# Down- and output projection of three segments in row tiles that rotate over four PSUM banks, with score fills between them

## The chip, the cores and the metric

The kernel runs on one core of a Trainium2 chip. The metric is the device time of one execution in microseconds, the median of the runs.

## The reference

Two branches work on the same input `x` of 2048 rows and 512 columns (`A_x`); their sum is weighted by a gate per row. Branch A is Infini-attention in four segments of 512 rows with 32 heads of 16 columns, with a running memory `M`, `z` per head. Branch B is a GEGLU feed-forward with 1792 hidden columns.

```python
for s in range(4):                                  # branch A, per segment
    logits = q_s @ k_s.T * 0.25 + causal_mask        # 32 heads, 512 x 512
    a_dot = softmax(logits) @ v_s
    a_mem = (phi(q_s) @ M) / (phi(q_s) @ z + 1e-6)   # phi(t) = t + 1 if t > 0 else exp(t)
    o_s = sigmoid(beta) * a_mem + (1 - sigmoid(beta)) * a_dot
    M, z = M + phi(k_s).T @ v_s, z + phi(k_s).sum()
a = o @ wo
b = (gelu(x @ w_gate) * (x @ w_up)) @ w_down          # branch B
g = sigmoid((x * gate_w).sum(-1))
out = g * a + (1 - g) * b
```

## The kernel before

All work is cut into named tasks, and each of the five queues (TensorE `pe`, ScalarE `act`, VectorE `dve`, GpSimd `pool`, and the DMA queue `sp`) runs its tasks in an order that is written out by hand in `ORDER`. `Sched.schedule` walks these lists only to hand out PSUM banks and to interleave the queues for bookkeeping; its estimates (`SWITCH`, `HOP`, `BLOCK`) do not appear in the program that runs. `Emitter` then derives the semaphore waits from what each instruction reads and writes. Between two TensorE instructions it sets none, as they run in order.

Names say what a task does; the first number is the segment.

- `K`, `Q`, `V` are the projections, `G` and `U` the gate and up projection of one hidden tile of 128 columns. Each has four matmuls over the contraction, in pieces of two (`.0`, `.2`), each matmul 128 by 128 by 512 columns. The results go to one of four PSUM banks `psW`, and ScalarE or VectorE copies them out (`Kev`, `Gev`, `Um` and so on). `gelu` tasks run on ScalarE between the attention phases, since the exponential and gelu need different tables.
- `qk{s}_{t}{A0,B0,L,A1,B1}` is a score fill. Four row tiles of 32 rows (one per head pair group) write into the four banks of `psXALL`, 512 columns each. One exponential `exp` on ScalarE reads all four banks into `pt`, and GpSimd masks the diagonal (`msk`). There are 18 fills a segment, and `psXALL` is held once, so a fill waits for the exponential before it.
- `pv{s}_{t}_{j}` is P times V in column tiles, with transpose `pvt` and normalization `norm` on VectorE into `oT`; `mz` updates the memory in column tiles; `numx` and `num` read it (`numx` in row tiles). `oTd` are DMA transposes of the memory part into `oT`.
- `D{s}_{tile}.{i}` is the joint down- and output projection of 128 rows of the segment: 4 matmuls of `oT` with `wo` and 14 of `hT` with `wd`, 18 in all, accumulated in one `psW` bank; before the change each tile goes through its 18 chunks in nine pieces of two, and the tiles run spread over the next segment's attention. `fin{s}_{tile}` scales the bank by `omgt` into `ostage` on ScalarE or VectorE, and `out` writes it.

TensorE thus works in three tilings: full (128 by 128), row tiles (32 by 128, in the profile `32*128`) and column tiles (`128*32`, `128*17`). `column_runs` looks at each stretch between two row-tiled tasks; where it holds a `pv` or `mz`, the full matmuls of the stretch are also issued as four column tiles each (line 533), so that the stretch has one tiling. Otherwise they are issued as one (line 531).

Segment 3 keeps its own form: its last tile `D3_3` is accumulated in `psXALL` after all scores are done.

Of the kernel before, what the change touches and what calls it, by code (L numbers as in the profile page):

```python
# [16 lines left out]
D = 512  # L17
# [9 lines left out]
N_OST = 3  # L27
PSUM_KEYS = ("X", "W")
# [3 lines left out]
SWITCH = 0.097  # L32
# [54 lines left out]
    ),  # L87
    "act": (
# [15 lines left out]
    ),  # L104
    "dve": (
# [34 lines left out]
    ),  # L140
}
GAP = {DVE: 0.012, POOL: 0.063}
HOP = {PE: 0.25, ACT: 0.07, DVE: 0.07, POOL: 0.10, SP: 0.0}


class Instr:
# [64 lines left out]
class Sched:  # L211
# [48 lines left out]
    def schedule(self):  # L260
# [13 lines left out]
        while len(order) < n:  # L274
# [26 lines left out]
            if e == PE:  # L301
                if st < COLD:
                    t.finish = st + 2 * t.est[e] if 2 * t.est[e] <= COLD - st else COLD + t.est[e] - (COLD - st) / 2
                if t.tiled != mode:
                    t.finish += SWITCH
# [898 lines left out]
```

## Time and profile before

| what | us |
|---|---|
| median of 3 runs (264.21 to 264.8) | 264.63 |
| the profiled execution, own time | 265.65 |
| its span, first to last instruction | 264.4 |
| TensorE busy (matmul) | 259.4 (98%) |
| ScalarE busy | 212.2 (80%) |
| VectorE busy | 196.6 (74%) |
| GpSimd busy | 106.0 (40%) |
| granted TensorE clock | 1.00 |

The profiled execution lies 1.02 us above the median. Matmuls are pipelined, so a matmul's duration is longer than the distance to the next one's start; busy time of TensorE counts any stretch in which one is under way. Line numbers are those of the kernel before. Line 531 is a full matmul, 533 a column-tiled part of one, 906 a score fill, 912 its exponential, 954 and 962 P times V, 873 the memory update, 826 its row-tiled reading, 1053 the multiplication of the up projection into `hT`, 1099 and 1102 the scaled copies of the output.

### The profile page before, as it was taken

The numbers are of one execution on the slowest core, as the hardware profiler recorded it, in microseconds if no ns is written. First come the engines' busy times: TensorE is split into PE (matmuls) and PEld (weight loads), VectorE is DVE, ScalarE is ACT, GpSimd is POOL, SyncE is SP. The second block draws the span as 40 slices with busy tenths as digits, with TensorE's granted clock in tenths as the row PEclk, the third lists the DMA queues.
The fourth block names the chain that finished last, engine by engine and source line by source line (L and its number), as shares of the span: only waits on it lengthen the run. The fifth ranks groups of instructions, "written<-read, shape, count | busy, mean of one in ns | idle before, by whom it ended". The sixth has DMA issues, their size and how long they took to land.

```text
span 264.4 us, 9416 instructions
## 1 busy us (share of the span) xinstructions
PE 259.4 (98%) x4164; PEld 120.0 (45%) x4164; DVE 196.6 (74%) x369; ACT 212.2 (80%) x190; POOL 106.0 (40%) x256
## 2 busy tenths in 40 slices
PE   8799999999999999999999999999999999999996
PEld 4444445344544444544444444543455434454454
DVE  1589998898998978767795877679895765637363
ACT  3589999889999798799968888789986786877822
POOL 8216843815003464461460164256460233316520
PEclk9999999999999999999999999999999999999999
DMA  6973033940006956120003413310002031000102
GB/s 217 282 198 62 4 72 101 331 141 2 5 6 166 170 84 61 44 82 0 2 2 85 71 32 62 103 41 1 4 2 42 2 84 44 12 30 2 42 2 82
DMA packets 32776, 18.37 MB, mean 69 GB/s; under 512 B 20576, under 2 KB 32736, under 8 KB 32736
## 3 DMA queue, kind: packets, MB, share of 16 engines
q1 hardware_dynamic: 31632, 16.73, 27.5%
q10 hardware_dynamic: 1104, 1.05, 1.2%
q8 instruction: 32, 0.52, 0.8%
q14 instruction: 8, 0.07, 0.1%
HBM read 9.84 MB, written 2.10 MB: 45 GB/s over the span
## 4 chain that ended last, share of the span: by engine, by line
PE 91%; DMA 3%; DVE 2%; POOL 2%; ACT 1%; issue 1%; ACTq 0%; DVEq 0%
PE psW L531 47%; PE psW L533 25%; PE psXALL L906 9%; PE psW L954 5%; DMA wk<-in_A_wk_dram 3%; PE psXALL L533 1%; PE psW L962 1%; PE psXALL L531 1%; POOL gbd L681 1%; ACT pt L912 1%; PE psXALL L826 1%; DVE mzbd L892 1%; PE psW L873 0%; POOL pt L915 0%; DVE obf L984 0%
## 5 line engine op out<-in xcount | busy, mean ns | idle before, releaser
L912 ACT ACTIVATE pt<-psXALL 128x2048 bf16<-128x2048 f32 x64 | 120.1, 1876 | 23.2 <-PE psXALL L906 19.8
L915 POOL TENSOR_SCALAR_AFFINE_SELECT pt<-pt 128x256 bf16<-128x256 bf16 x128 | 57.3, 457 | 119.9 <-ACT pt L912 114.9
L1053 DVE TENSOR_TENSOR hT<-psW,hT 128x512 bf16<-128x512 f32 x56 | 37.6, 686 | 19.0 <-PE psW L531 15.0
L968 DVE STREAM_TRANSPOSE tb<-psW 128x512 f32<-128x512 f32 x32 | 22.3, 707 | 19.5 <-PE psW L962 19.3
L531 PE MATMUL psW<-wd,hT 128*128 128x512 bf16 x136 | 35.5, 380 | 0.0
L531 PE MATMUL psW<-xT,wu 128*128 128x512 bf16 x132 | 34.9, 380 | 0.0
L531 PE MATMUL psW<-xT,wg 128*128 128x512 bf16 x138 | 34.0, 379 | 0.0
L915 POOL TENSOR_SCALAR_AFFINE_SELECT ptl<-ptl 128x512 bf16<-128x512 bf16 x32 | 23.2, 726 | 10.9 <-ACT ptl L912 9.3
L906 PE MATMUL psXALL<-qT,kpad 32*128 32x320 bf16 (+3 forms) x512 | 25.4, 273 | 0.0
L533 PE MATMUL psW<-xT,wu 128*32 128x512 bf16 x368 | 22.0, 379 | 0.0
L533 PE MATMUL psW<-xT,wg 128*32 128x512 bf16 x344 | 20.9, 379 | 0.0
L1037 ACT ACTIVATE hT<-psW 128x512 bf16<-128x512 f32 x28 | 15.3, 598 | 6.6 <-PE psW L533 3.5
L813 POOL COPY exsT<-exs 32x4 f32<-32x4 f32 x64 | 14.1, 220 | 15.9 <-ACT exs L804 12.2
L531 PEld LDWEIGHTS psW<-xT,wg 128*128 128x128 bf16 x138 | 12.9, 98 | 16.0 <-DVE hT L554 0.5
L531 PEld LDWEIGHTS psW<-wd,hT 128*128 128x128 bf16 x136 | 12.5, 98 | 15.8 <-issue 2.1
L533 PE MATMUL psW<-wd,hT 128*32 128x512 bf16 x296 | 19.4, 380 | 0.0
L954 PE MATMUL psW<-pt,vaug 128*17 128x192 bf16 (+3 forms) x512 | 19.3, 273 | 0.0
L531 PE MATMUL psW<-xT,wk 128*128 128x512 bf16 (+1 forms) x74 | 17.2, 334 | 2.0 <-DMA wk<-in_A_wk_dram 1.5
L906 PEld LDWEIGHTS psXALL<-qT,kpad 32*128 32x128 bf16 x512 | 7.6, 92 | 24.7 <-ACT pt L912 14.0
L912 ACT ACTIVATE ptl<-psXALL 128x2048 bf16<-128x2048 f32 x8 | 15.0, 1878 | 4.6 <-PE psXALL L906 4.6
L531 PEld LDWEIGHTS psW<-xT,wu 128*128 128x128 bf16 x132 | 11.7, 98 | 14.7 <-issue 1.9
L531 PE MATMUL psW<-wv,xT 128*128 128x512 bf16 x58 | 16.5, 380 | 0.0
(122 smaller groups left out, 372.3 us busy)
## 6 DMA issues: line engine op xcount, KB each, us to landing
out_dram<-ost SPq DMA_DIRECT2D x15, 128.0 KB, 1.8
wg<-in_B_w_gate_dram SPq DMA_DIRECT2D x2, 896.0 KB, 7.9
wu<-in_B_w_up_dram SPq DMA_DIRECT2D x2, 896.0 KB, 7.0
wd<-in_B_w_down_dram SPq DMA_DIRECT2D x2, 896.0 KB, 5.7
phkt<-in_A_x_dram SPq DMA_DIRECT2D x3, 512.0 KB, 3.8
vlow<-vaug SPq DMA_DIRECT2D x8, 136.0 KB, 2.7
hT<-in_A_x_dram SPq DMA_DIRECT2D x2, 256.0 KB, 3.9
wq<-in_A_wq_dram SPq DMA_DIRECT2D x2, 256.0 KB, 6.1
```

What stands on the lines that cost most here:

```text
L531: return e.matmul(view(), lhsT, rhs, start=first, stop=last)
L533: r = e.matmul(view()[c:c + 32, :], lhsT[:, c:c + 32], rhs, start=first, stop=last, tile_position=(0, c))
L681: gb = task("gbd", POOL, [Instr(lambda e, c=c, j=j: e.tensor_tensor(gbd[32 * c:32 * c + 32, :, j, 0:16], gmat[32 * c:32 * c + 32, 2 * c + ...
L813: cross = task(f"exsT{s}", POOL, [Instr(lambda e, g=g, c=c: e.tensor_copy(exsT[sl][32 * g:32 * g + 32, c:16:4], exs[32 * c:32 * c + 32, s4 ...
L826: task(f"numx{s}", PE, [Instr(lambda e, g=g, i=i, qt=qt, t=t: e.matmul(X[g][:, 34 * i:34 * i + 34], phq[32 * g:32 * g + 32, t, qt * 128:(q ...
L906: instrs.append(Instr(lambda e, g=g, lhs=lhs, rhs=rhs, c0=c0, ncol=ncol: e.matmul(X[g][:, c0:c0 + ncol], lhs(32 * g), rhs(32 * g), start=T ...
L912: exp_task(s, f"exp{s}_{t}{name}", [Instr(lambda e: e.activation(dst[:], XALL[:, :].rearrange("p (g c) -> p g c", g=4), ACTF.Exp, scale=AT ...
L915: task(f"msk{s}_{t}{name}", POOL, [Instr(lambda e, view=view, pat=pat, base=base: e.affine_select(out=view, in_=view, compare_op=ALU.is_ge ...
L954: instrs.append(Instr(lambda e, t=t, q=q, kb=kb, slot=slot, c0=c0: e.matmul(gp.f32()[32 * q:32 * q + 17, 128 * kb + 64:512], Vaug[sl][:, k ...
L968: task(f"pvt{s}_{t}_{j}", DVE, [Instr(lambda e: e.transpose(Tb[:, j, :], gp.f32()[:, :]), [gp.key], [("Tb", j)], dve_t(512))], grp=gp)
L1037: lambda e, g=g, ft=ft, s=s: e.activation(hT[s % 2][:, ft, :], g.f32()[:, :], ACTF.Gelu_apprx_tanh),
L1053: task(f"Um{s}_{ft}", DVE, [Instr(lambda e, g=g, ft=ft: e.tensor_tensor(hT[sl][:, ft, :], g.f32()[:, :], hT[sl][:, ft, :], ALU.mult), [g.k ...
```

## The change

For segments 0 to 2 the tiles no longer accumulate one after the other. `row_downs` takes all four banks at once, one per tile. The first two and the last two of the 18 chunks of each tile stay whole matmuls (`D{s}_{tile}.0` and `.16`). The 14 chunks between are cut into four row parts of 32 contraction rows. In step `k` of four, row group `r` works on tile `(r + k) % 4`, so that the four row groups always write four different banks; each piece `R{s}.{step}.{c}` covers two chunks, 8 matmuls. After each step the groups take the next bank; the first matmuls of a step wait on TensorE's own semaphore (`own`) for the matmuls of the step before. As `R` pieces have the tiling of score fills, fills stand between them in the new order without a change of tiling.

The orders of all five queues are written anew. A block now lies in the first third of the next segment's attention, where the up projections of the next segment stood; these move behind it. All other functions keep what they compute. `finish` is the old end of `downs`, moved out. The constants of `Sched` change as well.

```diff
+D_HEAD, D_TAIL = 2, 2
-SWITCH = 0.097
+SWITCH = 0.1
 ...
     "pe": (
 ...
+        "U0_6.2 U1_4.0 U1_4.2 Q2_1.2 U0_13.0 pv0_3_1 U0_13.2 qk1_0B0 D0_1.0 Q2_3.0 Q2_3.2 D0_3.0 qk1_0L D0_0.0 "
+        "D0_2.0 R0.0.2 R0.0.4 qk1_0A1 R0.0.6 R0.0.8 R0.0.10 R0.0.12 R0.0.14 qk1_0B1 R0.1.2 R0.1.4 R0.1.6 R0.1.8 "
+        "R0.1.10 R0.1.12 R0.1.14 qk1_1A0 R0.2.2 R0.2.4 R0.2.6 R0.2.8 R0.2.10 R0.2.12 R0.2.14 qk1_1B0 R0.3.2 R0.3.4 "
+        "R0.3.6 R0.3.8 R0.3.10 qk1_1A1 R0.3.12 R0.3.14 D0_0.16 D0_2.16 D0_1.16 qk1_1B1 pv1_0_1 pv1_0_0 U1_9.0 "
+        "U1_9.2 U1_8.0 qk1_2A0 Q2_2.0 Q2_2.2 D0_3.16 U1_2.0 U1_8.2 qk1_2B0 U1_2.2 U1_11.0 U1_11.2 pv1_1_1 pv1_1_0 "
 ...
+        "qk2_0A0 V2_1.0 Q3_1.0 Q3_1.2 V2_1.2 D1_0.0 D1_3.0 D1_2.0 D1_1.0 R1.0.2 qk2_0B0 R1.0.4 R1.0.6 R1.0.8 "
 ...
+        "G3_12.0 G3_12.2 G3_13.0 G3_13.2 U3_3.0 qk3_0A0 U2_2.0 U3_3.2 U2_2.2 D2_0.0 D2_3.0 D2_1.0 D2_2.0 R2.0.2 "
+        "qk3_0B0 R2.0.4 R2.0.6 R2.0.8 R2.0.10 R2.0.12 R2.0.14 qk3_0L R2.1.2 R2.1.4 R2.1.6 R2.1.8 R2.1.10 qk3_0A1 "
+        "R2.1.12 R2.1.14 R2.2.2 R2.2.4 R2.2.6 qk3_0B1 R2.2.8 R2.2.10 R2.2.12 R2.2.14 R2.3.2 qk3_1A0 R2.3.4 R2.3.6 "
+        "R2.3.8 R2.3.10 R2.3.12 R2.3.14 qk3_1B0 D2_0.16 D2_1.16 D2_2.16 V3_3.0 V3_3.2 qk3_1A1 U3_5.0 U3_5.2 "
 ...
-HOP = {PE: 0.25, ACT: 0.07, DVE: 0.07, POOL: 0.10, SP: 0.0}
+HOP = {PE: 0.235, ACT: 0.07, DVE: 0.07, POOL: 0.10, SP: 0.0}
 ...
                 if d[0] == "c":
-                    if d[1] == PE and eng == PE:
+                    if d[1] == PE and eng == PE and not ins.own:
                         continue
 ...
+    def row_downs(s):
+
+        sl = s % 2
+        gs = tuple(Grp(banks) for _ in range(4))
+
+        def chunk(c, tile):
+            at = slice(tile * 128, (tile + 1) * 128)
+            if c < 4:
+                return oT[sl][:, c, at], wo[:, c, :], [("oT", sl, tile, c), ("w", "wo")]
+            return hT[sl][:, c - 4, at], wd[:, c - 4, :], [("hT", sl, c - 4), ("w", ("wd", (c - 4) // 7))]
+
+        def whole(tile, c0, c1):
+            g = gs[tile]
+            return [mm(g, lambda: g.f32()[:, :], *chunk(c, tile), c == 0, c == 3 + NFT, 512) for c in range(c0, c1)]
+
+        def part(r, tile, c):
+            a, b, rd = chunk(c, tile)
+            return Instr(lambda e: e.matmul(gs[tile].f32()[:, :], a[32 * r:32 * r + 32, :], b[32 * r:32 * r + 32, :],
+                                            start=False, stop=False, tile_position=(32 * r, 0)),
+                         rd, [gs[tile].key], mm_t(512) / 4)
+
+        for tile in range(4):
+            task(f"D{s}_{tile}.0", PE, whole(tile, 0, D_HEAD), grp=gs[tile])
+        c1 = 4 + NFT - D_TAIL
+        for step in range(4):
+            for c in range(D_HEAD, c1, 2):
+                ins = [part(r, (r + step) % 4, cc) for cc in range(c, min(c + 2, c1)) for r in range(4)]
+                t = Task(f"R{s}.{step}.{c}", {PE: ins}, grp=gs)
+                t.tiled, t.row = "qk", True
+                if c == D_HEAD and step > 0:
+                    t.hand = True
+                    for i in ins[:4]:
+                        i.own = True
+                S.add(t)
+        for tile in range(4):
+            task(f"D{s}_{tile}.{c1}", PE, whole(tile, c1, 4 + NFT), grp=gs[tile])
+        for tile in range(4):
+            finish(s, tile, gs[tile])
 ...
     def downs(s):
         sl = s % 2
         last = s == NSEG - 1
+        if not last:
+            return row_downs(s)
```

The scaled copies move as well: of the twelve `fin` tasks of segments 0 to 2, ScalarE runs three (`fin0_1`, `fin2_1`, `fin2_3`) and VectorE nine.

More of the change, by code (lines that the diff above doesn't have):

```diff
@@ L142 @@
 GAP = {DVE: 0.012, POOL: 0.063}
-HOP = {PE: 0.25, ACT: 0.07, DVE: 0.07, POOL: 0.10, SP: 0.0}
+HOP = {PE: 0.235, ACT: 0.07, DVE: 0.07, POOL: 0.10, SP: 0.0}
 class Instr:
-    __slots__ = ("fn", "reads", "writes", "est", "dma_sem", "waits", "deps", "inc", "fence", "wide", "cols")
+    __slots__ = ("fn", "reads", "writes", "est", "dma_sem", "waits", "deps", "inc", "fence", "wide", "cols", "own")
     def __init__(self, fn, reads=(), writes=(), est=0.1, dma_sem=None):
@@ L161, in __init__ @@
         self.fence = False
-        self.wide = self.cols = False
+        self.wide = self.cols = self.own = False
 class Grp:
@@ L190, in __init__ @@
         self.alts = alts
-        self.grps = () if grp is None else (grp,)
+        self.grps = () if grp is None else grp if isinstance(grp, tuple) else (grp,)
         self.after = tuple(after)
@@ L195, in __init__ @@
         self.tiled = None
+        self.row = self.hand = False
         self.table = None
@@ L281, in schedule @@
                     continue
-                st = max(cur[e], ready_at[t.id])
+                st = max(cur[e] + (SWITCH if e == PE and t.tiled != mode else 0.0), ready_at[t.id])
                 if t.grps and t.grps[0].bank is None:
@@ L303, in schedule @@
                     t.finish = st + 2 * t.est[e] if 2 * t.est[e] <= COLD - st else COLD + t.est[e] - (COLD - st) / 2
-                if t.tiled != mode:
-                    t.finish += SWITCH
                 mode = t.tiled
@@ L332, in schedule @@
                 npred[s.id] -= 1
-                hop = 0.0 if (e == PE and s.alts.keys() == {PE}) else HOP[e]
+                hop = 0.0 if e == PE and s.alts.keys() == {PE} and not (t.row and s.hand) else HOP[e]
                 ready_at[s.id] = max(ready_at[s.id], avail + hop)
@@ L390, in finalize @@
             for d in ins.deps:
-                if d[0] == "c" and (d[1] != PE or eng != PE):
+                if d[0] == "c" and (d[1] != PE or eng != PE or ins.own):
                     top[d[1]] = max(top.get(d[1], -1), d[2])
@@ new lines, in finish @@
+    def finish(s, tile, g):
+        gt = 4 * s + tile
+        ost = ostage[gt % N_OST]
+        rd, wr = [g.key, ("omgt", s)], [("ost", gt % N_OST)]
+        f = S.add(Task(f"fin{s}_{tile}", {
+            ACT: [Instr(lambda e: e.activation(ost[:], g.f32()[:, :], ACTF.Copy, scale=omgt[:, gt:gt + 1]), rd, wr,
+                        act_t(512, ap=True))],
+            DVE: [Instr(lambda e: e.tensor_scalar(ost[:], g.f32()[:, :], omgt[:, gt:gt + 1], None, ALU.mult), rd, wr,
+                        dve_t(512, ap=True))]}, grp=g))
+        if s == NSEG - 2:
+            fins.append(f)
+        dma(f"out{gt}", SP, lambda: out[0, gt * 128:(gt + 1) * 128, :], lambda: ost[:], wr, [("hbm", gt)], 131072,
+            issue=0.47, sm=sem_out[gt])
@@ L1096, in downs @@
             pieces(f"D{s}_{tile}", g, ins, 2, after=dep)
-            rd = [key, ("omgt", s)]
-            f = S.add(Task(f"fin{s}_{tile}", {
-                ACT: [Instr(lambda e, view=view, gt=gt, tile=tile: e.activation(
-                    ostage[(4 * s + tile) % N_OST][:], view(), ACTF.Copy, scale=omgt[:, gt:gt + 1]), rd,
-                    [("ost", (4 * s + tile) % N_OST)], act_t(512, ap=True))],
-                DVE: [Instr(lambda e, view=view, gt=gt, tile=tile: e.tensor_scalar(
-                    ostage[(4 * s + tile) % N_OST][:], view(), omgt[:, gt:gt + 1], None, ALU.mult), rd,
-                    [("ost", (4 * s + tile) % N_OST)], dve_t(512, ap=True))]}, grp=g))
-            if s == NSEG - 2:
-                fins.append(f)
-            dma(f"out{gt}", SP, lambda gt=gt: out[0, gt * 128:(gt + 1) * 128, :],
-                lambda tile=tile: ostage[(4 * s + tile) % N_OST][:], [("ost", (4 * s + tile) % N_OST)], [("hbm", gt)], 131072, issue=0.47, sm=sem_out[gt])
+            finish(s, tile, g)
     fins = []
```

167 rows, old and new, of the table ORDER are left out of this document.

## The prediction

> **What bounds the kernel now.** I read the page first, then windows over the stages, then the chain of work that ended last, then the timeline around two score fills, then the waits.
>
> From the page, in turn: the span, the engines, the chain by line, and the groups of the exponential, of a weight-stationary matmul and of the two kinds of VectorE bank release:
>
> ```profile
> span 264.4 us, 9416 instructions
> PE 259.4 (98%) x4164; PEld 120.0 (45%) x4164; DVE 196.6 (74%) x369; ACT 212.2 (80%) x190; POOL 106.0 (40%) x256
> PE psW L531 47%; PE psW L533 25%; PE psXALL L906 9%; PE psW L954 5%; DMA wk<-in_A_wk_dram 3%; PE psXALL L533 1%; PE psW L962 1%; PE psXALL L531 1%; POOL gbd L681 1%; ACT pt L912 1%; PE psXALL L826 1%; DVE mzbd L892 1%; PE psW L873 0%; POOL pt L915 0%; DVE obf L984 0%
> ...
> L912 ACT ACTIVATE pt<-psXALL 128x2048 bf16<-128x2048 f32 x64 | 120.1, 1876 | 23.2 <-PE psXALL L906 19.8
> ...
> L531 PE MATMUL psW<-wd,hT 128*128 128x512 bf16 x136 | 35.5, 380 | 0.0
> ```
>
> TensorE is the chain nearly everywhere. Windows, cut at fills, say where it is not (columns: length, then busy time and instructions of each engine):
>
> ```profile
> core 0: us, PE busy (x) PEld busy (x) DVE busy (x) ACT busy (x) POOL busy (x), PEclk, DMA share, GB/s
> ...
> 14.86:61.16 46.30, 45.76 (x707) 19.61 (x706) 42.89 (x79) 42.34 (x41) 23.38 (x62) 1.00 0.48 122
> 61.16:83.73 22.57, 22.57 (x465) 11.12 (x463) 20.29 (x39) 22.16 (x17) 4.02 (x10) 1.00 0.11 20
> 83.73:264.40 180.67, 178.66 (x2929) 82.52 (x2925) 127.88 (x238) 140.51 (x123) 71.31 (x167) 1.00 0.22 48
> ```
>
> From 61 us on TensorE has no gap but the 2 us after its last matmul. Segment 0 (14.86 to 61.16) also loads VectorE to 93%, and that is where TensorE waits for banks:
>
> ```profile
> PEld psW L531 <- DVE hT L554: 1.1, 2, 0.6
> ...
> PEld psW L531 <- DVE kT L554: 0.9, 1, 0.9
> ```
>
> A busy TensorE is not one that streams. The chain in order of time (start, us, what) shows what a score fill costs:
>
> ```profile
> 65.74 12.20 PE psW L533 x224
> ...
> 86.82 0.34 PE psXALL L906 x32
> 87.17 2.27 PE psW L531 x10
> 89.43 0.33 PE psXALL L906 x8
> 89.77 2.26 PE psW L531 x10
> ```
>
> 224 column-tiled matmuls are 56 sets of four; less one switch of 0.1, 12.1 / 56 = 0.216 us for a set of 512 columns, as long as one full matmul. Ten full ones would be 2.16; the stretch behind a fill takes 2.27, so leaving row tiles costs 0.11. A fill is also 512 columns per row group, some 0.23, and takes 0.33 to 0.34: entering costs 0.10. A fill pays 0.21 us for its two switches.
>
> The timeline around two fills shows the tightest round, fill to fill:
>
> ```profile
> 168.59 0.40 PE L906 MATMUL psXALL<-qT,kpad 32*128 32x448 bf16 x8
> ...
> 169.04 1.88 ACT L912 ACTIVATE pt<-psXALL 128x2048 bf16<-128x2048 f32 x1 [0.79 <-PE psXALL L906]
> ...
> 170.97 0.40 PE L906 MATMUL psXALL<-qT,kpad 32*128 32x320 bf16 x8
> ```
>
> All four X banks are filled, read by one exponential, and filled again: 0.45 + 1.88 + 0.05 = 2.38 us at least, whatever TensorE has to do in between.
>
> **The change, part by part.** The sum is made against this execution (265.65 us, span 264.4), which lies 1.0 above the median, 264.63; I move the median by the same difference.
>
> *Switches.* In the order before, 72 fills and 3 row-tiled memory products stand alone between other matmuls: 75 row stretches, 150 switches. In the new order the row pieces join fills: R0 takes 5 fills (qk1_0A1 to qk1_1A1) into one stretch, R1 5 (qk2_0B0 to qk2_1A0), R2 6 (qk3_0B0 to qk3_1B0). That is 4 + 4 + 5 = 13 stretches fewer, 124 switches: 13 x 0.215 = **-2.8 us**, all on the chain. Bounds 2.6 to 2.9.
>
> *Row tiles in place of full ones.* 84 R pieces of 8 matmuls are 168 sets for 168 full matmuls. No row here shows a row-tiled accumulation over 512 columns. Nearest are the fills: the x32 line is 8 sets of 64 columns with 32 weight loads, and takes the 0.34 of the fill with two sets. So neither issue nor weight loads limit row tiles at 512 columns, and I take 0.216 a set: **0**. From single starts in the trace, a fill's first 448 columns take 0.200 where 448/512 of 0.216 is 0.189; were that paid by each set, it would be 168 x 0.011 = +1.9. Below zero is excluded, since the columns must stream. The Trainium skill, "TensorE: Matmul & The Clock Gate", Part 3 (packing small matmuls), gives four row tiles at K = 32 and N = 512 a speedup of 3.07, not 4, over one after the other. By it a set would take 0.281 (an estimate) and the sum would rise by 11 us; the x32 fill speaks against it. PE's instructions rise by 498 matmuls and as many loads, at a density that the x224 stretch ran for 12 us without a gap: 0.
>
> *Short rounds.* All banks of W are held by a block, so the new order packs rounds differently. From its rows: a piece (two matmuls) 0.432, fill 0.23, two switches 0.21. Five pieces with switches are 2.60, five R pieces without 2.39: both fill the 2.38. Four pieces are 2.17, and six such rounds stand in the new order (behind qk0_2A0, qk1_0B0, qk1_0L, qk2_1A0, qk2_1A1, qk3_2L): 6 x 0.21 = 1.26. Three rounds (behind qk0_1B1, qk1_2A1, qk2_2L) have three pieces and a memory product mz (0.5 us), 2.24: 3 x 0.14 = 0.42. The old order had about 0.1 of this. 1.26 + 0.42 - 0.1 is **+1.6**; bounds 1.2 (some coincide with bank waits) to 1.9. So over half of the switch time returns as waits for the exponential.
>
> *Hand-overs.* A step's first four matmuls wait on PE's own semaphore until the step before has left the banks; behind the waiting weight load stands all of PE's queue, fills too, and through them ScalarE. A matmul takes 0.380, the next would start after 0.216, and waking takes some 0.06 (the fill of 168.59 ends at 168.98 by its starts, its exponential starts at 169.04): 0.23 exposed. Of nine hand-overs seven have a fill between, 0.23 long, which covers them up to 0.04; R2.1.14 to R2.2.2 and R2.2.14 to R2.3.2 have nothing: 2 x 0.23 = **+0.45**, and 7 x 0.02 = **+0.15**. Bounds 0.3 and, with no cover, 9 x 0.25 = 2.2.
>
> *Edges of the blocks.* Four accumulators hold all four W banks for some 12 us. Into a block, the last D.0 needs the fourth bank, and R needs oT of all heads (the norm of tile 3). Out of it, the next projection waits for the first scaled copy: 0.23 (as at the hand-over) + 0.75 (a copy of line 1102 in the groups by line) + 0.05 (as from exponential to fill) = 1.03 behind the D.16. After R0 and R1 a fill and two or three pieces cover that. After R2, V3_3.0 follows D2_0.16 by two pieces, 0.86: **+0.2**. The covers are PE pieces of 0.432 and fills; without them each of six edges costs up to a VectorE operation, 0.7. Bounds 0 to 4.2. VectorE has no W bank to empty during R, so it comes out of the block without arrears; I stay near the low end.
>
> *Segment 0.* Its pieces sum to 45.2 in 46.30: 1.1 of waits, the two rows above. The new order puts K1_2 and K1_3, which waited, elsewhere. VectorE's load there is the same; I take **-0.4**, bounds -1.1 and +0.5.
>
> *Nothing else.* From segment 0 to 1 ScalarE runs gelus (22.16 of 22.57 us busy): the first exponential of segment 1 ended 21.8 behind the fill at 61.16 (at 82.97 in the trace). The new order has one copy of 0.5 less there, 21.3, and TensorE's own pieces from qk0_3B1 to qk1_0B0 sum to 21.7, so ScalarE stays covered; if not, up to 0.3. The tail after the last fill is still 10.5 us of PE work, with the mask of the last exponential landing about when pv3_3_1 comes up. out0 stands ahead of x3_0 and pkT1_0 in SP's queue; mz1, which needs them, comes five rounds later. Cost 0.
>
> Sum: -2.8 + 0 + 1.6 + 0.45 + 0.15 + 0.2 - 0.4 = -0.8. 265.65 becomes 264.85, the median **263.8 us**.
>
> **The rivals.**
>
> *Blocks starve for banks (slower).* If VectorE is one operation behind at the edges, each of the three blocks costs one more at its exit or entry, 0.75: 2.25 over my count, 266.1. It decides from 1.35 us on, where -0.8 becomes +0.53. For: a block holds every bank, and after it four scaled copies, P.V transposes (707 ns) and the multiply of the ups meet on VectorE. Against: the rest inside R.
>
> *It evens out.* Half of that, or short rounds and hand-overs at their upper bounds: 264.1 to 265.1.
>
> *Row sets are not pipelined when they accumulate.* Then a set takes its 0.380: 168 x 0.164 = +27.5, some 291 us. Against: fills stream at full rate, and full and column-tiled accumulation shows no penalty. By the page of the Trainium skill named above it would be 275 (an estimate).
>
> *Bank waits of segment 0 vanish* and swallow its short rounds: -2.8 + 1.2 + 0.45 - 1.1 = -2.2, 262.4.
>
> **How the numbers follow.** Forecast (263.1 to 264.1) 0.45; larger gain 0.08; even 0.19; starved blocks 0.24; unpipelined rows 0.04. A measurement of this kernel can tell about 0.2%, 0.53 us. Faster by more is 0.45 + 0.08 = 0.53, within 0.19, slower 0.24 + 0.04 = 0.28. The range reaches from the larger gain, 262.4, to the starved blocks, 266.2; outside remain the row rate, the worst edges and a little below. The forecast's own range is 263.1 to 264.1.
>
> **What would show it.** Row-tiled matmuls on wd start 0.216 apart per set; 0.226 or more would show the row-rate term. Fills inside R cost 0.23 with no 0.1 on either side. The nine short rounds are 2.38 to 2.43 long with TensorE waiting for the exponential. Gaps of 0.23 at two hand-overs in segment 2 and of 0.05 at most at the others. TensorE waits for `ost` (the scaled copies) at 0.2 us in all. I am wrong if the three R stretches hold gaps beyond these, if bank waits at their edges exceed 1 us, or if segment 0 waits for over 1.6 us.

## The result and the profile after

The kernel after takes 266.17 us (median of 6 runs, 265.74 to 266.33); the kernel before, run beside it, 264.43 (6 runs, 264.06 to 264.80). The ratio is 1.0063, 95% interval 1.0053 to 1.0074: the change loses 0.6%, some 1.7 us, where 0.8 us of gain was forecast. The profiled execution after took 265.74.

The page of the kernel after, the rows that answer to those of before (530 is now the full matmul, 532 the column-tiled, 905 the fill, 911 the exponential, 1073 a row-tiled `R` matmul):

```profile
span 264.5 us, 10396 instructions
...
PE 257.9 (97%) x4662; PEld 127.2 (48%) x4662; DVE 189.7 (72%) x364; ACT 217.1 (82%) x196; POOL 102.7 (39%) x256
...
PE 85%; ACT 7%; DMA 3%; DVE 2%; issue 1%; POOL 1%; ACTq 0%; DVEq 0%
PE psW L530 31%; PE psW L532 23%; PE psW L1073 14%; PE psXALL L905 8%; PE psW L953 5%; ACT pt L911 5%; ACT ptl L911 2%; DMA wv<-in_A_wv_dram 2%; PE psXALL L532 1%; DMA hT<-in_A_x_dram 1%; PE psW L961 1%; PE psXALL L825 1%; DVE mzbd L891 1%; POOL pt L914 1%; DVE hT L553 1%
...
L1073 PE MATMUL psW<-wd,hT 32*128 32x512 bf16 x576 | 34.5, 374 | 0.0
```

Two things are new in the chain: the exponential has 7% of it (1% before), and a load, `wv`, has 2%. The spans of the two profiled executions are equal, 264.4 and 264.5, although the medians lie 1.7 apart. That is an accident of the execution that was shown of before: in it, TensorE waited 1.47 us for `wk` in the first 10 us.

```profile
8.70 1.14 PE L531 MATMUL psW<-xT,wk 128*128 128x256 bf16 x9 [1.47 <-DMA wk<-in_A_wk_dram]
```

So I profiled the kernel before a second time (264.2 us, span 263.0, without that wait; "before, again" below), and cut every execution into a head, up to the first score fill, and a middle, from there to the start of the last matmul (both from single starts):

| kernel | first fill at | last matmul at | middle |
|---|---|---|---|
| before, as shown | 14.86 | 262.17 | 247.32 |
| before, again | 13.20 | 260.71 | 247.51 |
| after | 14.66 | 262.24 | 247.57 |

Against the undisturbed execution the head is 1.46 longer and the middle 0.06. All of the loss is in the head, where no `R` piece runs yet.

The chain of the kernel after in order of time, in the head:

```profile
6.68 1.47 PE psW L530 x13
...
8.24 0.01 ACT kpad L717
8.25 5.50 DMA wv<-in_A_wv_dram
...
13.80 0.93 PE psW L530 x5
14.73 0.33 PE psXALL L905 x8
```

and of before, again:

```profile
10.67 1.30 PE psXALL L531 x6
11.97 1.30 PE psW L531 x8
13.27 0.33 PE psXALL L906 x8
```

Before, TensorE works with no gap over 0.05 us up to its first fill, in the last line. After, it stands behind a load of `wv` that was issued only at 8.25. The timelines name the wait (start, us, engine, line, what; in brackets the idle time before it):

```profile
8.25 0.37 ACTq L567 DMA_DIRECT2D wv<-in_A_wv_dram  x1
...
13.80 0.60 PE L530 MATMUL psW<-wv,xT 128*128 128x512 bf16 x2 [1.34 <-DMA wv<-in_A_wv_dram]
```

```profile
5.06 0.37 ACTq L568 DMA_DIRECT2D wv<-in_A_wv_dram  x1
```

The second fence is before, again. `w_wv1`, the load of the second half of `wv`, is a step in ScalarE's order. Before, it stood behind the first copy of `x`; in the new order it stands behind four copies, the last of them `K0_0even` (line 717), which waits for the first K projection. Its issue moves from 5.06 to 8.25, its data land at 13.75 instead of 12.04, after the first half of V0_2, and TensorE loses 1.34 us there.

### The profile page after: what moved, and what is told of

The parts are those of the page before. It is cut to its first block, busy times and chain, and to the rows that moved or that the text cites. A ratio compares the mean times of both kernels' runs of the same rounds, so it can differ in the third digit from the quotient of the medians.

```text
span 264.5 us, 10396 instructions
## 1 busy us (share of the span) xinstructions
PE 257.9 (97%) x4662; PEld 127.2 (48%) x4662; DVE 189.7 (72%) x364; ACT 217.1 (82%) x196; POOL 102.7 (39%) x256
## 3 DMA queue, kind: packets, MB, share of 16 engines
q10 hardware_dynamic: 1104, 1.05, 1.2%
## 4 chain that ended last, share of the span: by engine, by line
PE 85%; ACT 7%; DMA 3%; DVE 2%; issue 1%; POOL 1%; ACTq 0%; DVEq 0%
PE psW L530 31%; PE psW L532 23%; PE psW L1073 14%; PE psXALL L905 8%; PE psW L953 5%; ACT pt L911 5%; ACT ptl L911 2%; DMA wv<-in_A_wv_dram 2%; PE psXALL L532 1%; DMA hT<-in_A_x_dram 1%; PE psW L961 1%; PE psXALL L825 1%; DVE mzbd L891 1%; POOL pt L914 1%; DVE hT L553 1%
## 5 line engine op out<-in xcount | busy, mean ns | idle before, releaser
L1073 PE MATMUL psW<-wd,hT 32*128 32x512 bf16 x576 | 34.5, 374 | 0.0
L530 PE MATMUL psW<-xT,wu 128*128 128x512 bf16 x118 | 29.8, 380 | 0.0
L532 PE MATMUL psW<-xT,wg 128*32 128x512 bf16 x472 | 27.3, 379 | 0.0
L532 PE MATMUL psW<-xT,wu 128*32 128x512 bf16 x424 | 26.6, 380 | 0.0
L530 PE MATMUL psW<-xT,wg 128*128 128x512 bf16 x106 | 25.7, 380 | 0.2 <-DVE hT L553 0.2
L1102 DVE TENSOR_SCALAR ost<-psW,omgt 128x512 bf16<-128x512 f32 x10 | 7.2, 747 | 23.9 <-PE psW L530 22.3
L1073 PEld LDWEIGHTS psW<-wd,hT 32*128 32x128 bf16 x576 | 19.6, 93 | 9.8
L905 PEld LDWEIGHTS psXALL<-qT,kpad 32*128 32x128 bf16 x512 | 9.2, 92 | 24.3 <-ACT pt L911 15.5
L532 PEld LDWEIGHTS psW<-xT,wg 128*32 128x32 bf16 x472 | 11.8, 97 | 11.1 <-issue 0.2
L953 PEld LDWEIGHTS psW<-pt,vaug 128*17 128x17 bf16 x512 | 11.5, 91 | 8.7 <-POOL exsT L812 0.4
```

The source lines that it names most:

```text
L530: return e.matmul(view(), lhsT, rhs, start=first, stop=last)
L532: r = e.matmul(view()[c:c + 32, :], lhsT[:, c:c + 32], rhs, start=first, stop=last, tile_position=(0, c))
L905: instrs.append(Instr(lambda e, g=g, lhs=lhs, rhs=rhs, c0=c0, ncol=ncol: e.matmul(X[g][:, c0:c0 + ncol], lhs(32 * g), rhs(32 * g), start=T ...
L953: instrs.append(Instr(lambda e, t=t, q=q, kb=kb, slot=slot, c0=c0: e.matmul(gp.f32()[32 * q:32 * q + 17, 128 * kb + 64:512], Vaug[sl][:, k ...
L1073: return Instr(lambda e: e.matmul(gs[tile].f32()[:, :], a[32 * r:32 * r + 32, :], b[32 * r:32 * r + 32, :], start=False, stop=False, tile_ ...
L1102: DVE: [Instr(lambda e: e.tensor_scalar(ost[:], g.f32()[:, :], omgt[:, gt:gt + 1], None, ALU.mult), rd, wr, dve_t(512, ap=True))]}, grp=g))
```

## Experiments

**The load alone, both ways.** Theory: the place of `w_wv1` in ScalarE's order is the loss. Rival: the row pieces and their rounds are.

```diff
 "act" of the kernel after                              (a_wv_early)
-tload w_wk0 w_wk1 w_wk2 w_wv0 x0ev0a_0 x0ev0b_0 x0ev1_1 K0_0even w_wv1
+tload w_wk0 w_wk1 w_wk2 w_wv0 x0ev0a_0 w_wv1 x0ev0b_0 x0ev1_1 K0_0even
 "act" of the kernel before                             (b_wv_late)
-x0ev0b_0 w_wv1 x0ev1_0 K0_1ev K0_0even K0_0ev
+x0ev0b_0 x0ev1_0 K0_1ev K0_0even w_wv1 K0_0ev
```

> The changed kernel with one token moved: w_wv1, the load of the second half of wv, is issued behind ScalarE's first copy of the head, as in before, instead of behind four. Theory 1 (the late load costs the head, 1.34 us of wait at V0_2.2): that wait is gone, first fill at 13.0 to 13.4 instead of 14.66, time 264.5 to 265.0, ratio to before 1.000 to 1.002. Theory 2 (the loss is made by the row blocks: short rounds, hand-overs, edges): 265.9 to 266.2, ratio 1.0055 to 1.007.

> The kernel before with the same token moved the other way: w_wv1 behind K0_0even. Theory 1: TensorE waits for wv at V0_2.2 by 1.2 to 1.6 us, time 265.5 to 266.0, ratio to before 1.004 to 1.006. Theory 2: 264.3 to 264.7, ratio 0.999 to 1.001.

> The kernel before once more, for a second profile of its head. The profiled execution of before lay 1.2 us above its median, with a wait of 1.5 us for wk ahead of the first fill. Theory 1 (that wait is not usual, and the usual head of before is shorter): no wait over 0.5 us for a weight load in the head, first score fill at 13.2 to 13.7 us instead of 14.86. Theory 2 (the profile shown is the usual one, and the loss lies in the row blocks): first fill at 14.6 to 15.0.

Measured: before, again has its first fill at 13.20 and no wait for a weight load. The kernel after with the early load takes 264.55 us (264.18 to 266.3), ratio to before 1.0003 (0.9987 to 1.002). The kernel before with the late load takes 266.47 (266.23 to 268.78), ratio 1.0086 (1.0054 to 1.0117). One token takes the loss away from the one (1.6) and gives it to the other (1.9 to 2.0). The kernel after came out as expected; the kernel before lost 0.5 more than the upper end of its expectation (266.0), and why it lost more is open. In the kernel after with the early load, V0_2 has no wait, and the first fill is at 13.03:

```profile
4.74 0.38 ACTq L567 DMA_DIRECT2D wv<-in_A_wv_dram  x1
...
12.17 0.59 PE L530 MATMUL psW<-wv,xT 128*128 128x512 bf16 x2
```

The profiled execution of the kernel before with the late load was its slowest (268.78), with a wait of 2.94 us for `wv` and a clock of 0.994; I use its median only. With the load in place, the rest of the change is worth nothing: 264.55 against 264.53.

**Row tiles against whole matmuls in the same order.** What is the row part worth by itself?

```diff
-                ins = [part(r, (r + step) % 4, cc) for cc in range(c, min(c + 2, c1)) for r in range(4)]
-                t = Task(f"R{s}.{step}.{c}", {PE: ins}, grp=gs)
-                t.tiled, t.row = "qk", True
 ...
+                task(f"R{s}.{step}.{c}", PE, whole(step, c, c + 2), grp=gs[step])
```

> The changed kernel in its own orders, with each R piece as two whole matmuls on one tile after the other in place of eight row parts: no hand-overs, but each fill within a block switches again. If the sum of the prediction is right in the middle part (13 pairs of switches 2.8, hand-overs 0.65 and some 0.1 of five-piece rounds): 2.0 slower than the changed kernel, 268.0 to 268.4, ratio to before 1.0135 to 1.015. If row tiles cost as much as they save: 265.7 to 266.4, ratio 1.005 to 1.0075.

> The kernel after, with the second half of wv issued behind the first copy, and with each R piece as two whole matmuls of its step in place of eight row tiles (no hand-over). Theory (row tiles save switches and pay for it with hand-overs and waits): 13 stretches more, 26 switches, cost 2.8; the hand-overs (0.75) and the 0.1 to 0.2 of waits that a round of five R pieces shows fall away; so 1.9 to 2.0 above the same kernel with row tiles (264.55), that is 266.5, a ratio to the kernel before of 1.0075. Rival (a set of four row tiles is itself cheaper or dearer than a full matmul of 512 columns): 0.01 us per set is 1.7, so 264.8 or 268.2.

Measured: `a_whole` (late load) 269.22 (268.5 to 270.38), ratio 1.0186 (1.0154 to 1.0217); `a_wv_whole` (early load) 266.9 (266.55 to 267.66), ratio 1.0099 (1.008 to 1.0117). Both are slower than expected (268.0 to 268.4, and 266.5). The middle of `a_wv_whole` is 250.00, that of `a_wv_early` 247.69. Of these 2.31, the rounds (fill to fill) of the three blocks make up 1.53. Another 0.81 stands in one round behind a block, that of qk2_2L, as a gap inside the memory update `mz2` (timeline of `a_wv_whole`):

```profile
175.08 0.22 PE L872 MATMUL psW<-vaug,phkt 128*32 128x34 bf16 x6 [0.82 <-issue]
```

`a_whole` has this gap too, behind the same 58th of the 64 matmuls, 1.05 long, and 1.59 in the blocks against the kernel after. No run with row tiles has it, and neither profile of before. The profile names nothing that TensorE waited for, and its cause is open. So row tiles save 1.5 to 1.6 where the blocks are; the medians are 2.35 apart. The chain of `a_wv_whole` over a step of block 0, and the same stretch of the kernel after:

```profile
92.97 0.33 PE psXALL L905 x8
93.31 3.13 PE psW L530 x14
```

```profile
85.47 0.47 PE psXALL L905 x32
...
86.03 1.89 ACT ptl L911
...
88.05 0.40 PE psXALL L905 x8
...
90.61 0.22 PE psXALL L905 x8
90.83 3.11 PE psW L1073 x56
```

14 whole matmuls and a fill take 3.46 from fill to fill, 14 sets of row tiles and a fill 3.27 by their starts (90.43 to 93.71; the chain lets a fill begin where the matmul before it ends, and has 3.33). The fill is 0.22 instead of 0.33, nothing is paid behind it, and the hand-over under it costs 0.04. 13 fills by the 0.21 of two switches are 2.73; the two hand-overs that stand alone take 0.5 of it back, three rounds of five `R` pieces 0.35 (see below), and the hand-overs under a fill some 0.2 to 0.3, which leaves 1.6. That is 0.3 to 0.4 less than expected; that the medians show 0.3 to 0.4 more goes, by the profiles, to the gap in `mz2`.

A set of row tiles that is dearer or cheaper by 0.01 is out: a round of six pieces that waits for nothing takes 2.81 in row tiles and 3.03 in whole matmuls, apart by its two switches alone. By the same middles and without the gap, the new orders without row tiles are 250.00 - 0.81 - 247.51 = 1.7 slower than the old. So the change is a set of orders that costs 1.7 and a tiling that earns 1.5. The lines of the kernel after show what the order costs: behind qk1_0L TensorE has four pieces, and then waits for the whole exponential.

**The same pieces dealt out anew.** Theory: TensorE waits for exponentials only because some rounds, fill to fill, are short, and others hold more than they need. Rival: another engine takes back what is gained. In all of these the load is early; only the order of TensorE changes, mostly by moving fills past one or two pieces. The edits, in part:

```diff
 a_cut12, segments 1 and 2
-qk1_0B0 D0_1.0 Q2_3.0 Q2_3.2 D0_3.0 qk1_0L D0_0.0 D0_2.0 R0.0.2 R0.0.4 qk1_0A1 R0.0.6 ... R0.0.14 qk1_0B1 R0.1.2 ...
+qk1_0B0 D0_1.0 Q2_3.0 Q2_3.2 D0_3.0 D0_0.0 qk1_0L D0_2.0 R0.0.2 ... R0.0.8 qk1_0A1 R0.0.10 ... R0.1.4 qk1_0B1 R0.1.6 ...
-qk1_2A1 V2_3.2 mz1 U1_5.0 K2_2.0 qk1_2B1
+qk1_2A1 V2_3.2 mz1 U1_5.0 K2_2.0 U1_13.0 qk1_2B1
-qk2_1A0 R1.3.12 R1.3.14 D1_0.16 D1_1.16 qk2_1B0
+qk2_1A0 R1.3.12 R1.3.14 D1_0.16 D1_1.16 D1_3.16 qk2_1B0
-qk2_2B0 U2_10.0 K3_1.2 U2_10.2 pv2_1_1 pv2_1_0 qk2_2L mz2 Q3_2.0 Q3_2.2 U2_3.0 qk2_2A1
+qk2_2B0 U2_10.2 pv2_1_1 pv2_1_0 mz2 Q3_2.0 qk2_2L Q3_2.2 U2_3.0 U2_3.2 K3_0.0 U2_5.0 qk2_2A1
 a_cut13b, segment 3 (segment 1 as above, segment 2 as in the kernel after)
-qk3_0L R2.1.2 ... R2.1.10 qk3_0A1 R2.1.12 R2.1.14 R2.2.2 ... R2.2.6 qk3_0B1 R2.2.8 ... R2.2.14 R2.3.2 qk3_1A0
+qk3_0L R2.1.2 ... R2.1.14 qk3_0A1 R2.2.2 ... R2.2.10 qk3_0B1 R2.2.12 R2.2.14 R2.3.2 ... R2.3.6 qk3_1A0
-qk3_1B0 D2_0.16 D2_1.16 D2_2.16 V3_3.0 V3_3.2 qk3_1A1
+qk3_1B0 D2_2.16 D2_1.16 V3_3.0 V3_3.2 U3_5.0 qk3_1A1
```

> The kernel after, with the early load, and with the same pieces dealt out anew between the score fills of segments 1 and 2, so that eight short rounds (behind qk1_0B0, qk1_0L, qk1_2A1, qk2_1A0, qk2_1A1, qk2_2L and two beside them) hold five pieces each. Theory (TensorE waits there for the exponential because the round is too short): the waits of 0.27 + 0.47 + 0.11 + 0.31 + 0.27 + 0.14 = 1.57 go, one hand-over that lost its fill (R0.0.14 to R0.1.2) costs 0.25: 264.55 - 1.3 = 263.2, ratio 0.995. Rival (ScalarE or VectorE set the pace of these segments, so a wait that is taken from one round comes back in another): no change, 264.5, ratio 1.000.

> As a_cut12, and segment 3 dealt out anew too: the step R2.1 ends at a fill, D2_3.16 stands ahead of V3_3.0, the round behind qk3_2L holds five pieces, and two pieces fewer are left behind the last fill, where the column-tiled pieces of D3_3w1 move ahead of the pieces that need the last oT. Theory: waits of 0.21 (round of qk3_0L), 0.22 (hand-over now under a fill), 0.27 (V3_3.0 for its bank) and 0.23 (round of qk3_2L) go: 0.9 below a_cut12, 262.3, ratio 0.9915. Rival (the tail behind the last fill is set by exponential, mask, P.V and norm, so two pieces fewer there leave TensorE idle for 0.86): no better than a_cut12, 263.2.

> The kernel after with the early load, segment 1 dealt out as in a_cut12, segment 2 left as the change has it, and in segment 3 only what asks for no bank ahead of time: R2.1 ends at a fill, D2_2.16 stands first after the block and U3_5.0 is pulled into that round, and the piece is given back in the round behind qk3_2A0; the tail is as in the kernel after. Theory (TensorE's waits can be taken away where the pieces that fill a short round need no bank that VectorE or ScalarE still holds): segment 1 gains the 0.55 that its stretch of a_cut12 showed, segment 3 0.21 + 0.22 + 0.27 less 0.28 of new waits, 0.42; 264.55 - 0.97 = 263.6, ratio 0.9965. Rival (whatever is gained is given back at the next bank): 264.5, ratio 1.000.

> As a_cut13b, and in segment 2 the pieces behind qk2_1A0 to qk2_3A1 one or two places earlier, so that the short rounds behind qk2_1A0, qk2_1A1 and qk2_2L are filled, while mz2 and Q3_2.0 stay on two sides of the fill qk2_2L. Theory: 0.31 + 0.27 + 0.14 less 0.1 to 0.2, so 0.55 below a_cut13b: 263.0, ratio 0.9945. Rival (banks of W: pieces that come earlier stand and wait for copies of VectorE and ScalarE, whose places in their own orders have not changed, as in a_cut12, where segment 2 lost 0.7): no better than a_cut13b, 263.6 or more.

| kernel | median (range), us | ratio to before (95%) | middle | expected |
|---|---|---|---|---|
| a_wv_early | 264.55 (264.18 to 266.3) | 1.0003 (0.9987 to 1.002) | 247.69 | 264.5 to 265.0 |
| a_cut12 | 265.2 (264.73 to 265.7) | 1.0028 (1.0016 to 1.0041) | 248.15 | 263.2 |
| a_cut123 | 266.2 (265.79 to 266.58) | 1.0067 (1.0051 to 1.0083) | 248.65 | 262.3 |
| a_cut13b | 263.72 (263.39 to 264.16) | 0.9978 (0.9968 to 0.9988) | 247.02 | 263.6 |
| a_best | 264.13 (263.76 to 265.0) | 0.9992 (0.998 to 1.0003) | 247.25 | 263.0 |

`a_cut12`, `a_cut123` and `a_best` missed: each came out where its rival said, or above it. Each short round that was filled lost its wait for the exponential: the round behind qk2_1A0 takes 2.65 with five pieces where it took 2.48 with four, that behind qk1_0L 2.62 instead of 2.66. Segment 1 became 0.55 shorter. But in segment 2 of `a_cut12`, 1.02 longer, the pieces came earlier than the banks. Its chain goes over VectorE at two places (line numbers are smaller by 2 in this kernel: 528, 530, 903, 965 and 1050 are 530, 532, 905, 967 and 1052 of the kernel after):

```profile
170.97 0.73 DVE tb L965
...
171.74 0.61 PE psW L530 x8
...
174.14 0.70 DVE hT L1050
...
174.88 0.61 PE psW L528 x2
```

`Q3_2.0` and `U2_5.0`, one and two places earlier, wait for the four banks that VectorE empties in its unchanged order: the rounds behind qk2_2B0 and qk2_2L wait 0.50 and 0.52 (by my sums). `a_cut123` runs into the same in segment 3, 0.92 in the round behind qk3_2L; its stretch behind the last fill is 0.86 shorter, as the theory said, so the rival about the tail is out.

`a_cut13b` moves only pieces that need no bank ahead of time, and came out 0.1 from its expectation in time: 0.2% under the kernel before, its interval clear of 1. Part of that is luck: the kernel before ran 0.16 faster beside it than beside `a_wv_early`, and the expected ratio, 0.9965, lies just outside the interval. The middle gained 0.67 of the 0.97 expected (segment 1 the 0.55, segment 3 0.25 of 0.42).

`a_best` adds segment 2 without the bank conflicts. The rounds behind qk2_1A0, qk2_1A1 and qk2_2L lose 0.70 of waits in it, but 0.51 come back behind qk2_3B0, where `pv2_2_0`, now the first piece of the round, waits for GpSimd's mask and a V piece behind it for a bank:

```profile
182.79 0.61 PE L951 MATMUL psW<-pt,vaug 128*17 128x448 bf16 x16 [0.31 <-POOL pt L912]
```

Another 0.36 come back behind the last fill of segment 2, at 199.18. The waits of the weight loads (188 to 204) name what the G piece there waits for, VectorE's reading of the memory part out of a W bank (line 852, done at 199.12):

```profile
PEld psW L530 <- DVE phkt L852: 0.3, 1, 0.3
```

The rival holds for segment 2, the theory for segment 1 and in part for segment 3.

## Why the prediction was wrong

The direction failed at one step: **"Nothing else ... Cost 0"**. That paragraph looked at the gelu stage, the tail and SP's queue, and not at ScalarE's queue before the first fill, where the change moves a load behind three more instructions. Measured: +1.46 in the head, 1.6 to 1.7 by the medians with the load moved back. A DMA in a compute engine's order is issued when its turn comes, and its turn came 3.2 us later; the landing moved by some 1.7 (12.04 to 13.75). "DMA: Bandwidth & Descriptors" of the Trainium skill (Anatomy of one DMA, on the path of GpSimd) says that any semaphore wait happens on the issuing sequencer before dispatch. This trace, of a load on ScalarE's path, fits that: the issue at 8.25 stands right behind the start of the copy of line 717 at 8.24, which had waited 0.92 us for TensorE. The diff showed the move in its first line of `act`. No rival held it either: all four were about the middle. That starved blocks were put at 266.1, close to the 266.17 measured, is chance: the one wait at a block's edge is 0.27. And without the late load the kernel is even with before (264.55), not 0.8 faster, so the sum for the middle failed too; its terms follow.

The anchor hid it. I read the execution that was shown as typical "plus 1.0"; the plus was a wait for `wk` in the same 15 us. The question which wait made it slower than the median could have led to the head.

The other terms, against before, again:

- *Switches*, -2.8: right. A fill within `R` costs 0.22, and the three rounds of six `R` pieces are 0.22 shorter than the same rounds of whole matmuls (2.81 against 3.03). 13 times the 0.215 of the prediction is 2.79.
- *Row tiles in place of full ones*, 0: right. 48 row-tiled matmuls, 12 sets, take 2.59 us, 0.216 a set, as long as a full matmul:

```profile
209.64 2.59 PE psW L1073 x48
```

  The 3.07 of "TensorE: Matmul & The Clock Gate", Part 3 of the Trainium skill, by which the sum would have been 11 us worse, does not hold for this stream: four row tiles of 32 rows take as long as one whole matmul.
- *Short rounds*, +1.6: the mechanism right, the size low. By the starts of single matmuls the nine rounds wait 2.09 in all, where 1.68 was reckoned. The three with `mz` wait the 0.42 that was said; the six of four pieces wait 1.67 instead of 1.26, since 2.38 was read off one round, and five of the six have a longer floor (the shortest time that fill, exponential and next fill allow), up to 2.58; its parts are in the last section. And "five R pieces without switches are 2.39: both fill the 2.38" held for one round in a row stretch, that behind qk1_0A1 (2.38), whose fill had itself waited. Three others are 2.42, 2.48 and, behind an `L` fill, 2.61 long: 0.35 of waits that the sum did not hold.
- *Hand-overs*, +0.45 and +0.15: 0.25 and 0.26 at the two without cover, 0.04 to 0.09 at the four under a fill whose round waits for nothing else. Right within 0.1 to 0.2. Waits of the weight loads, whole kernel:

```profile
PEld psW L1073 <- PE psW L1073: 1.1, 2, 0.6
```

  (Weight loads run ahead of the matmuls, so their idle time is longer than the loss; from one set's start to the next it is 0.47 instead of 0.22.)
- *Edges of the blocks*, +0.2: 0.27 behind qk3_1B0, none elsewhere. Right, and the rival of starved blocks is out.
- *Segment 0*, -0.4: the direction right, the size low. Its waits, without its two short rounds counted above, are 0.6 instead of 1.28 (as shown) or 1.48 (again): -0.7 to -0.9.

Against before, again, this adds up: -2.79 for the switches, 2.09 for the nine rounds, 0.35 for the row rounds, 0.51 and some 0.2 for the hand-overs, 0.27 for the edge, -0.88 for segment 0, and 0.18 for a wait for a bank at 67.98, between segments 0 and 1, make -0.07. The middle measured 0.06 more, of which 0.11 is one K piece that the new order leaves behind the first fill. So TensorE's waits rose by as much as the switches gave, and the middle evens out. The terms that were too low are the nine rounds by 0.5, the row rounds by 0.35, and hand-overs, edges and the bank at 67.98 by some 0.35; segment 0 gave 0.5 more than said.

## What to carry to other kernels

When an order of queues is written anew, list every DMA in it with the instruction it now stands behind, compute engines' queues first and the head of the kernel above all; one load that moved three places cost twice what the tiling was forecast to gain. When one part of a change is taken out to price it, look where the difference stands: 0.8 of the 2.31 here stood in one gap outside the blocks. Before a trace is used as an anchor, ask what makes it differ from the median: a wait of its own is in the wrong place to be carried over. And where an engine has a floor per round, time that is taken out of a round is worth nothing until work from a richer round stands in it, and that work must find its bank, its mask and its place in the other engines' orders.

## What the runs showed of the hardware

- The floor of a round has three parts: from the fill's first matmul to the exponential, the 1.88 us of the exponential, and from its end to the next fill. In the kernel after, where ScalarE is free, the first part is 0.45 us among full or column-tiled work (0.49 for an `L` fill, 32 matmuls). It is 0.06 longer (0.51, and 0.55 for `L`) where the trace has a semaphore instruction of ScalarE right before the exponential; this is so behind qk1_0B0, qk1_0L, qk2_1A0 and qk2_1A1. Within a stretch of row tiles, behind a set without a wait, it is 0.49 without such an instruction and 0.50 to 0.55 with it. For `L` it is 0.59 there, and its 32 matmuls of 64 columns take 0.31 instead of 0.22 from first to last start. The third part, where TensorE waits for it, is 0.05, or 0.14 where the trace has a semaphore instruction of TensorE in between, as at 87.94 and 214.57. In `a_wv_early`:

```profile
210.54 0.50 PE L905 MATMUL psXALL<-qT,klow 32*128 32x64 bf16 x32
...
211.13 1.88 ACT L911 ACTIVATE ptl<-psXALL 128x2048 bf16<-128x2048 f32 x1 [1.02 <-PE psXALL L905]
...
213.15 0.40 PE L905 MATMUL psXALL<-qT,kpad 32*128 32x448 bf16 x8
```

  (2.61 from fill to fill is 0.59 + 1.88 + 0.14, with five row pieces that take 2.40.) So a part of what is saved at the switch is paid at the exponential; why a fill behind row tiles takes longer to release it, no run tests.
- Four row tiles that write four different banks, 512 columns each, stream at the rate of one full matmul, 0.216 us, for 12 to 14 sets on end, with a weight load for each tile, and score fills between them cost only their columns.
- The load of 256 KB on ScalarE's queue takes 5.5 us (after), 7.0 us (before, again) and 8.2 us (before, as shown) from issue to landing in the first 15 us, while the core's DMA engines move 300 to 330 GB/s; issued 3.2 later, it landed 1.7 later.
